# A steady block in a new order: the next block's early products in one group among the output products instead of two

## The chip, the cores and the metric

The kernel runs on one core of one Trainium2 chip. The metric is device time in microseconds of one execution on that core. Before the change three runs gave 2297.81, 2297.93 and 2298.03 us, so the median is 2297.93 us. One further execution was profiled; all durations below come from it.

## The reference

The input `x` is 8 sequences of 4096 tokens with 192 channels. First a causal convolution over 7 taps runs along each sequence, with one set of 7 softmax weights for each of 8 heads of 24 channels. Its result is 32768 tokens of 192 channels, which go through two matrix products with a SiLU between them. All of it is float32.

```python
w = np.exp(w); w = w / (np.sum(w, axis=-1, keepdims=True) + 1e-09)
x_unf = x_pad[:, idx, :].reshape(B, S, K, H, group)
out = np.einsum('hk,bskhg->bshg', w, x_unf)
...
h = x @ w_in                        # 192 -> 2048
g = h * (1.0 / (1.0 + np.exp(-h)))
return (g @ w_out)                  # 2048 -> 192
```

## The kernel before

**Blocks.** The 32768 tokens are cut into 32 blocks of 1024, and each block into two halves of 512. Channels lie on partitions. The convolution of a block is done by ScalarE, which scales shifted copies of the input (`v` steps, lines 542 and 545), and by accumulating DMAs that GpSimd issues (line 546). DMAs issued by SyncE (`sp` steps, line 572) spread its result over both halves of the 128 partitions as the tile `dup`, and VectorE forms sums of it (`w` steps, `win`, lines 589 and 592).

**Input products.** The product with `w_in` has 192 = 3 x 64 rows to sum over, so each TensorE product uses a 64-row half of the array, 64\*128. The kernel does not multiply plainly: in 5 groups of three 128-column chunks, 15 products per group (`P0` to `P14`, line 684) on sums of inputs and of weights take the place of 18. The one chunk left over is done plainly (`L`, line 701). `P8.2` is product 8 of group 2. The upper and lower 64 rows, called A and B here, work at the same time; the order of products goes in pairs, one of A and one of B. In float32 each product is two passes, so a trace shows two matmul records for each.

**Chains.** The products of a group accumulate into three chains, each in a PSUM bank of its own (`CHAINS`, `CHAIN_BANKS`). In the middle of a chain its value is read out. A `u` step (ScalarE copy, line 733) takes chain 0; an `X`, `a` or `b` step (VectorE add or subtract, line 727) takes chain 1 or 2. The next product of that chain may start only when the read is done. For instance chain 0 is products 5, 2, 6, 1, 0, 14, and `u4` copies it after product 2, so product 6 waits for `u4`. Chain 1 is products 3, 9, 7, 4, 8, and `a1` reads it after product 4, so product 8 waits for `a1`. `S` steps apply SiLU (ScalarE, line 745).

**Output products.** The product with `w_out` has 20 products `Q0` to `Q19`, each for 4 slices of its sum (line 820), on sums of `g` that VectorE and GpSimd form (`t` steps, line 809). They use column halves of the array, 128\*64, again two at a time. Copies and sums combine them (`O`, `C`, `d` on ScalarE, lines 855 and 857; `m` on VectorE, line 868), VectorE turns the result (`o`, line 876), SyncE stores it (`st`, line 884).

**The order.** The string `PLAN` lists the steps of one steady block, and the loop at line 1096 goes through it once for each block `b`. A sign ahead of a step moves it to another block: `-` is block b-1, `=` b-2, `~` b-3, `+` b+1, `*` b+2, none is b itself. Every instruction is pinned, so each engine runs its own steps in the order of this string, and waits on semaphores hold back the one at its head. `START` and `FINISH` list the steps of the first and last blocks. Most of block b-1's input products stand in the first half of the string, its output products in the second half. Ten of block b's products come early: `P5.4 P5.0 L.00 P2.4 P2.0 P3.4 P6.4 L.01 L.02 P6.0`. In the steady order of before, TensorE's own steps are: 76 input products (73 steps, since three `L.1x` steps make two each; the last three are P5.4, P5.0 and `-P8.2`, with P5.4 two steps ahead of P5.0), 8 output products, 4 input products (L.00, P2.4, P2.0, P3.4), 16 output products, 4 input products (P6.4, L.01, L.02, P6.0), 56 output products. Each place where input and output products meet is called a switch here; there are six in a block.

Of the kernel before, what the change touches and what calls it, by code (L numbers as in the profile page):

```python
# [17 lines left out]
def kernel(  # L18
# [59 lines left out]


    PLAN = (  # L80
# [24 lines left out]
    )  # L105
    START = (
# [20 lines left out]
    )  # L127
    QUEUE = (0, 4, 1, 2, 3)
    CHAIN_BANKS = (
        (5, 4, 2, 3, 3),  # L130
        (7, 5, 0, 1, 6),
        (0, 6, 4, 7, 2),
    )
    XBANKS = {
        2: (1, 1, 4, 7, 0),
        4: (1, 0, 6, 6, 0),
    }
    PLAIN_BANKS = (0, 0, 2)
    OUT_BANKS = {"DX": 7, "DY": 2, "D2": 1, "D3": 4, "DC": 2}

    def pin(ins):
        return tc.keep_in_program_order(ins)
# [211 lines left out]
    def combine(g, e):  # L354
# [47 lines left out]
        (("x", 3), ("o", 0), "-", ("x", 1)),  # L402
        (("o", 10), ("o", 9), "-", ("o", 10)),
        (("o", 9), ("o", 9), "-", ("x", 3)),
        (("o", 11), ("o", 11), "+", ("o", 9)),
        (("x", 4), ("o", 8), "-", ("o", 11)),
        (("o", 3), ("o", 0), "+", ("o", 3)),
        (("o", 0), ("o", 0), "+", ("o", 7)),
        (("x", 5), ("o", 6), "+", ("x", 4)),
        (("o", 6), ("o", 6), "-", ("o", 0)),  # L410
        (("o", 5), ("o", 5), "+", ("o", 8)),
        (("x", 7), ("o", 2), "+", ("x", 1)),
        (("o", 8), ("o", 1), "-", ("o", 8)),
        (("o", 2), ("o", 2), "+", ("o", 8)),
        (("o", 7), ("o", 7), "n", ("o", 7)),
        (("o", 10), ("o", 11), "-", ("o", 10)),
        (("x", 6), ("o", 3), "-", ("x", 4)),
        (("x", 0), ("x", 0), "n", ("x", 0)),
    )
    OUT_FORMS = {  # L420
# [187 lines left out]
    def rows(t, e):  # L608
        return t[R * e : R * e + R]
# [54 lines left out]
    def plain_bank(b, i):  # L664
        return banks[PLAIN_BANKS[i]]

# [144 lines left out]
    def out_bank(node):  # L811
        name, e = OUT_HOME[node]
        return rows(banks[OUT_BANKS[name]], e)

# [15 lines left out]
    def mid(i):  # L830
        if not mids:
            cmb = xpool.tile([P, 4, TB], F32, tag="cmb", name="cmb")
            mids.extend(cmb[:, c, :] for c in range(4))
            mids.extend(xpool.tile([P, TB], F32, tag="yx", name="yx", bufs=2) for _ in range(2))
            mids.append(xpool.tile([P, TB], F32, tag="m4", name="m4"))
        return mids[i]
# [22 lines left out]
    def out_sum(b, i):  # L859
# [4 lines left out]
            lambda: (out_bank("Y"), rows(mid(2), 1)),  # L864
            lambda: (banks[OUT_BANKS["D3"]], mid(1)),
            lambda: (banks[OUT_BANKS["D2"]], mid(0)),
        )[i]()
# [264 lines left out]
```

## Time and profile before

| What | Before |
|---|---|
| Median of 3 runs | 2297.93 us |
| The profiled execution's own time | 2298.43 us |
| Span of its instructions on the core | 2296.4 us |
| Mean granted TensorE clock | 0.999 |
| DMA engines, mean rate over the span | 106 GB/s |

The span runs from the first to the last instruction, and the rest of the execution's time lies around it. In the timeline each row has the start, the length (from the first start to the last end where several instructions are merged), the engine, the source line, the operation and what it writes and reads. Matmul records are 0.59 us long but start 0.43 us after one another on a half of the array, as they are pipelined. So starts are to be compared, not ends. PEld is the loading of weights for a matmul.

### The profile page before, as it was taken

How to read it: one execution, taken by the hardware profiler on the slowest of the kernel's cores; microseconds unless marked ns; L12 is line 12 of the kernel's file. 1: busy time of each engine (PE TensorE's matmuls, PEld its weight loads, DVE VectorE, ACT ScalarE, POOL GpSimd, SP SyncE). 2: the span in 40 equal slices, each digit the busy share in tenths (PEclk: the TensorE clock that was granted, in tenths of full speed). 3: DMA queues.
4: the chain of work that ended last, by engine and by line, in shares of the span. 5: the costliest groups of instructions: out<-in, count | busy, mean ns of one | idle time of the engine just before them, and what ended most of it. 6: DMA issues, size and time to landing. Idle time of an engine off the chain costs nothing.

```text
span 2296.4 us, 31730 instructions
## 1 busy us (share of the span) xinstructions
PE 2288.8 (100%) x10622; PEld 930.8 (41%) x10622; DVE 2004.8 (87%) x2265; ACT 1554.2 (68%) x2842; POOL 656.2 (29%) x734
## 2 busy tenths in 40 slices
PE   9999999999999999999999999999999999999998
PEld 4344433344433444333444334443345443344433
DVE  8888889888888988889888889888898888898887
ACT  6377766677666776667776667766677766677543
POOL 5762222322223322223222232222232222322200
PEclk9999999999999999999999999999999999999999
DMA  7665566755567665667655676656676557765411
GB/s 166 106 108 101 98 104 118 131 105 104 95 117 128 117 106 96 108 118 128 106 101 95 121 129 111 105 98 110 120 126 105 96 99 124 129 108 94 75 30 19
DMA packets 527139, 244.22 MB, mean 106 GB/s; under 512 B 431936, under 2 KB 437056, under 8 KB 526976
## 3 DMA queue, kind: packets, MB, share of 16 engines
q0 software_dynamic: 76480, 140.02, 35.9%
q1 hardware_dynamic: 446272, 101.65, 24.9%
q8 instruction: 84, 1.38, 0.2%
q10 hardware_dynamic: 4224, 0.52, 0.2%
q14 instruction: 79, 0.65, 0.1%
HBM read 31.46 MB, written 25.17 MB: 25 GB/s over the span
## 4 chain that ended last, share of the span: by engine, by line
PE 100%; DVE 0%; issue 0%; ACT 0%; ACTq 0%
PE ps L820 47%; PE ps L684 45%; PE ps L701 3%; PE ps L901 2%; PE ps L625 2%; PE ps L1010 1%; PE ps L463 0%; DVE yx L876 0%; DVE cmb L868 0%; ACT u L733 0%; PE ps L489 0%; DVE zeros L149 0%; DVE warm L149 0%; ACTq L733 0%; ACT g L750 0%
## 5 line engine op out<-in xcount | busy, mean ns | idle before, releaser
L546 POOL DMA_DIRECT2D nat<-u x528 | 453.0, 930 | 1238.6 <-ACT u L545 798.8
L820 PE MATMUL ps<-g,wall 128*64 128x512 f32 x1984 | 743.8, 596 | 0.0
L684 PE MATMUL ps<-win,wr 64*128 64x512 f32 x1550 | 684.7, 598 | 0.0
L684 PE MATMUL ps<-win,ws 64*128 64x512 f32 x1550 | 644.1, 592 | 0.3 <-ACT u L733 0.3
L733 ACT COPY u<-ps 128x512 f32<-128x512 f32 x775 | 439.5, 590 | 114.7 <-issue 58.9
L820 PE MATMUL ps<-g,wx 128*64 128x512 f32 x1240 | 415.2, 593 | 0.0
L684 PE MATMUL ps<-dup,wr 64*128 64x512 f32 x868 | 401.4, 590 | 0.0
L820 PE MATMUL ps<-t,wall 128*64 128x512 f32 x992 | 369.2, 594 | 0.0
L545 ACT ACTIVATE u<-xt,taps 128x512 f32<-128x512 f32 x528 | 357.7, 716 | 0.7
L684 PEld LDWEIGHTS ps<-win,wr 64*128 64x128 f32 x1550 | 256.8, 186 | 215.3 <-issue 129.1
L727 DVE TENSOR_TENSOR g<-u,ps 128x512 f32<-128x512 f32 x465 | 309.5, 682 | 32.1 <-PE ps L684 29.9
L820 PEld LDWEIGHTS ps<-g,wall 128*64 128x64 f32 x1984 | 216.0, 137 | 222.3 <-issue 213.0
L684 PEld LDWEIGHTS ps<-win,ws 64*128 64x128 f32 x1550 | 257.3, 187 | 119.4 <-issue 92.2
L745 ACT ACTIVATE g<-g 128x512 f32<-128x512 f32 x465 | 280.9, 631 | 34.4 <-DVE g L727 34.4
L745 ACT ACTIVATE g<-ps 128x512 f32<-128x512 f32 x465 | 279.9, 602 | 29.2 <-PE ps L684 28.5
L727 DVE TENSOR_TENSOR ps<-u,ps 128x512 f32<-128x512 f32 x310 | 214.9, 693 | 92.7 <-ACT u L733 33.7
L684 PE MATMUL ps<-dup,ws 64*128 64x512 f32 x682 | 270.1, 590 | 0.0
L820 PE MATMUL ps<-t,wx 128*64 128x512 f32 x744 | 267.3, 595 | 0.0
L809 DVE TENSOR_TENSOR t<-g 128x512 f32<-128x512 f32 (+1 forms) x186 | 240.9, 1309 | 4.3
L855 ACT COPY cmb<-ps 64x512 f32<-64x512 f32 x124 | 72.1, 581 | 236.4 <-PE ps L820 210.0
L809 DVE TENSOR_TENSOR t<-g,t 128x2048 f32<-128x2048 f32 x93 | 212.9, 2289 | 8.0 <-PE ps L820 6.8
L820 PEld LDWEIGHTS ps<-g,wx 128*64 128x64 f32 x1240 | 129.6, 137 | 211.0 <-issue 210.1
(103 smaller groups left out, 2477.0 us busy)
## 6 DMA issues: line engine op xcount, KB each, us to landing
nat<-u POOLq DMA_DIRECT2D x528, 256.0 KB, 4.2
dup<-nat SPq DMA_DIRECT2D x345, 128.0 KB, 2.5
nat<-in_x_dram SPq DMA_DIRECT2D x382, 64.0 KB, 3.9
out_dram<-yx SPq DMA_DIRECT2D x244, 64.0 KB, 2.2
out_dram<-cmb SPq DMA_DIRECT2D x122, 64.0 KB, 4.5
raw<-in_moe_w_out_dram SPq DMA_DIRECT2D x8, 384.0 KB, 4.4
g<-in_moe_w_in_dram SPq DMA_DIRECT2D x8, 192.0 KB, 5.5
ws<-wr POOLq DMA_DIRECT2D x8, 192.0 KB, 5.2
```

The lines of the kernel that those rows point to most:

```text
L545: pin(nc.scalar.activation(z, src, AF.Copy, scale=tap))
L546: pin(nc.gpsimd.dma_start(out=dst, in_=z, accum_op=ALU.add))
L625: nc.tensor.matmul(hs[a, n, e], rows(wr[j], e)[:, a, k, :], rows(d, e)[:, n, k, :], start=k == 0, stop=k == NK - 1,)
L684: nc.tensor.matmul(to[:, cols], raw(g, *LEFT[e][r], e), rhs[:, cols], start=first, stop=True, skip_group_check=True,)
L701: nc.tensor.matmul(plain_bank(b, n and 1 + e)[:, cols], rows(wr[j] if own == e else ws[j], e)[:, a, k, :], rows(dups[b], e)[:, SLOT[e][2 * ...
L727: pin(nc.vector.tensor_tensor(out_, u, v, op=op))
L733: pin(nc.scalar.copy(us[b, g, o][:, cols], t1[:, cols]))
L745: pin(nc.scalar.activation(h, src, AF.Silu))
L809: pin(engine.tensor_tensor(g_part(to, js), g_part(u, js), g_part(v, js), op=op))
L820: nc.tensor.matmul(out_bank(node), out_form(OUT_FORMS[r])[:, j, :], g_part(OPERAND[r], j), start=first, stop=True, skip_group_check=True,)
L855: pin(nc.scalar.copy(to(), out_bank(node)))
L901: nc.tensor.matmul(banks[DOWN_BANKS[k]][R * n : R * n + R, :], wo[j][:, a, e, R * k : R * k + R], g_tile(b, j, a)[:, n, e, :], start=j == ...
```

## The change

`PLAN` is a new order of the same 331 steps. In TensorE's order, the input products of a block now stand as 76 and 8: L.00 moves into the long section, `-P8.2` out of it into the short one, and the 4 + 4 early products of before become one group of 8 with it. The output products stand as 8 and 72 instead of 8, 16 and 56. The signs of many steps change with it, because the point of the string at which a block begins lies elsewhere. The `t`, `v`, `S`, `d`, `m`, `o` and `sp` steps are in new places too. Some chains, `X` sums, the plain chunk and two output sums get other PSUM banks. Three sums of output weights, formed once per run, are in a new order. `START`, `FINISH` and the functions are as they were. The diff, cut to the places where input and output products meet in the order, and the banks:

```diff
     PLAN = (
...
-        "-P11.2 -P10.3 -S1.1 -b1.2 -S3.3 -P4.2 -P8.3 -S1.3 -S0.1 -b5.3 -P10.2 P5.4 sp.0 -S1.0 "
-        "-S3.2 sp.2 -a1.2 P5.0 -a0.3 -S5.3 -b5.2 -P8.2 -Q4.3 -S1.2 +v.04 -Q17.1 -Q17.3 -Q4.2 "
-        "-a0.2 +v.15 -S5.2 -S4.2 -Q4.1 u5.0 -Q17.2 -tC4 w.0 u5.4 -Q4.0 -Q17.0 -O.0 L.00 w.1 "
-        "-C.0 P2.4 -tC3 -tD2 P2.0 P3.4 +v.23 +v.02 u4.0 u4.4 -S0.2 -Q5.1 -Q16.3 -Q3.2 -Q16.0 "
...
-        "+v.05 -Q6.2 +v.13 -t6 -Q16.2 -t5 -d.H -Q3.3 -Q12.0 *ld.0 -t7 +v.06 -t8 P6.4 L.01 -O.1 "
-        "-t9 L.02 P6.0 -Q6.1 -Q18.2 -Q15.2 -Q18.3 -Q15.1 -Q18.0 -Q11.3 -Q15.0 -t10 -Q13.1 "
...
+        "-u0.2 -P0.3 -tB1 -P9.2 -a1.1 -S2.3 -a5.3 -S5.1 -P0.2 -P11.3 -tC2 -P8.1 -u1.3 -S2.2 "
+        "-P12.3 -S1.0 -a0.1 -u1.2 -P14.3 -X4.2 -b1.3 -P14.2 -S0.0 -S1.1 -P12.2 -S4.3 sp.1 "
+        "-P4.3 -P7.2 -P11.2 -S3.2 -S3.3 +v.20 -b1.2 -P10.3 P5.4 -a1.3 -S4.2 -a5.2 -P10.2 -b5.3 "
+        "=st.2 -P8.3 -b5.2 -S5.3 sp.0 u5.4 -P4.2 sp.2 L.00 -a1.2 -a0.3 -S5.2 -S1.3 P5.0 u5.0 "
+        "+v.23 -Q4.1 -Q17.0 -Q4.3 -tC3 w.0 +v.14 -S0.1 -Q17.2 -Q17.3 -Q4.2 +v.01 -S1.2 w.1 "
+        "-Q17.1 -tD2 -Q4.0 -C.0 -P8.2 P2.4 -tC4 u4.4 L.01 P2.0 u4.0 P6.4 L.02 P6.0 P3.4 -O.0 "
+        "-Q3.3 -Q12.0 -Q5.0 -tD4 u2.0 -Q12.1 -tD3 +v.16 -Q12.2 +v.26 -S0.3 -a0.2 *ld.1 -Q5.1 "
...
     CHAIN_BANKS = (
-        (5, 4, 2, 3, 3),
-        (7, 5, 0, 1, 6),
-        (0, 6, 4, 7, 2),
+        (3, 4, 5, 2, 5),
+        (7, 3, 4, 1, 6),
+        (0, 6, 7, 0, 0),
     )
     XBANKS = {
-        2: (1, 1, 4, 7, 0),
-        4: (1, 0, 6, 6, 0),
+        2: (1, 1, 0, 7, 0),
+        4: (1, 0, 3, 6, 2),
     }
-    PLAIN_BANKS = (0, 0, 2)
-    OUT_BANKS = {"DX": 7, "DY": 2, "D2": 1, "D3": 4, "DC": 2}
+    PLAIN_BANKS = (0, 0, 5)
+    OUT_BANKS = {"DX": 7, "DY": 2, "D2": 4, "D3": 1, "DC": 2}
```

More of the change, by code (lines that the diff above doesn't have):

```diff
@@ L404 @@
         (("o", 9), ("o", 9), "-", ("x", 3)),
+        (("o", 5), ("o", 5), "+", ("o", 8)),
         (("o", 11), ("o", 11), "+", ("o", 9)),
@@ L410 @@
         (("o", 6), ("o", 6), "-", ("o", 0)),
-        (("o", 5), ("o", 5), "+", ("o", 8)),
         (("x", 7), ("o", 2), "+", ("x", 1)),
@@ L414 @@
         (("o", 2), ("o", 2), "+", ("o", 8)),
+        (("x", 6), ("o", 3), "-", ("x", 4)),
         (("o", 7), ("o", 7), "n", ("o", 7)),
         (("o", 10), ("o", 11), "-", ("o", 10)),
-        (("x", 6), ("o", 3), "-", ("x", 4)),
         (("x", 0), ("x", 0), "n", ("x", 0)),
```

35 rows, old and new, of the table PLAN are left out of this document.

## The prediction

> **What bounds the kernel now.** I read the page's busy shares first, then its chain of waits.
>
> ```profile
> span 2296.4 us, 31730 instructions
> PE 2288.8 (100%) x10622; PEld 930.8 (41%) x10622; DVE 2004.8 (87%) x2265; ACT 1554.2 (68%) x2842; POOL 656.2 (29%) x734
> PE 100%; DVE 0%; issue 0%; ACT 0%; ACTq 0%
> L505 DVE STREAM_TRANSPOSE xt<-nat 128x512 f32<-128x512 f32 x96 | 63.0, 682 | 0.6 <-DMA nat<-in_x_dram 0.6
> ```
>
> TensorE is busy all through, and the chain that ended last lies on it alone. The transposes count the blocks: 96, three each, so 32. No matmul is added or taken away by the change. So only time in which TensorE runs below its pace can be won, and I looked for it in the timeline of TensorE alone, at the places where input products (L684, L701) and output products (L820) meet. A half of the array starts a pass every 0.43 us there (1057.16 to 1059.73 are six steps, 0.428 each), whatever the kind of product. The columns are start and length in us, engine, line, operation. The first stretch holds the end of the long input section with P8.2, and the second the group L.00, P2.4, P2.0, P3.4.
>
> ```profile
> 1054.68 0.59 PE L684 MATMUL ps<-dup,ws 64*128 64x512 f32 x1
> 1055.11 0.59 PE L684 MATMUL ps<-dup,ws 64*128 64x512 f32 x1
> 1055.12 1.02 PE L684 MATMUL ps<-dup,wr 64*128 64x512 f32 x2
> 1055.63 0.69 PE L684 MATMUL ps<-win,wr 64*128 64x512 f32 x1
> ...
> 1056.68 0.64 PE L820 MATMUL ps<-t,wall 128*64 128x512 f32 x1
> 1057.16 0.59 PE L820 MATMUL ps<-t,wall 128*64 128x512 f32 x1
> ...
> 1059.73 0.59 PE L820 MATMUL ps<-t,wall 128*64 128x512 f32 x1
> 1060.26 0.69 PE L701 MATMUL ps<-dup,ws 64*128 64x512 f32 x1
> 1060.80 0.59 PE L701 MATMUL ps<-dup,ws 64*128 64x512 f32 x1
> 1061.23 0.59 PE L684 MATMUL ps<-win,ws 64*128 64x512 f32 x1
> 1061.66 0.59 PE L684 MATMUL ps<-win,ws 64*128 64x512 f32 x1
> 1062.18 0.64 PE L820 MATMUL ps<-t,wx 128*64 128x512 f32 x1
> 1062.66 0.59 PE L820 MATMUL ps<-t,wx 128*64 128x512 f32 x1
> ```
>
> The starts tell two losses. Around a group of input products, from 1059.73 to 1062.66, are six steps of one half: 2.93 us, where six times 0.43 are 2.57. **A switch there and back costs 0.36 us**: 0.10 and 0.10 on the way to input products (0.53, 0.54 in place of 0.43), 0.09 and 0.05 on the way back (0.52, 0.48).
>
> At P8.2, from 1055.11 to 1057.16, are four steps that should take 0.43 + 0.43 + 0.52 + 0.48 = 1.86 us; they take 2.05. **P8.2 loses 0.19 us**: its first pass starts at 1055.63 in place of 1055.55, 0.08 late, and is itself 0.69 in place of 0.59 long, 0.10 more. What it waits for is on VectorE and in the weight loads:
>
> ```profile
> 1054.26 0.59 PE L684 MATMUL ps<-win,ws 64*128 64x512 f32 x1
> 1054.89 1.29 DVE L727 TENSOR_TENSOR g<-u,ps 128x512 f32<-128x512 f32 x2
> 1055.63 0.29 PEld L684 LDWEIGHTS ps<-win,wr 64*128 64x128 f32 x2
> 1053.39 0.59 PE L684 MATMUL ps<-dup,ws 64*128 64x512 f32 x1
> 1053.69 0.32 PEld L684 LDWEIGHTS ps<-win,wr 64*128 64x128 f32 x2
> 1053.82 0.59 PE L684 MATMUL ps<-win,wr 64*128 64x512 f32 x1
> L727 DVE TENSOR_TENSOR g<-u,ps 128x512 f32<-128x512 f32 x465 | 309.5, 682 | 32.1 <-PE ps L684 29.9
> L684 PEld LDWEIGHTS ps<-win,wr 64*128 64x128 f32 x1550 | 256.8, 186 | 215.3 <-issue 129.1 <-ACT u L733 43.8 <-ACT g L750 13.3
> ```
>
> P4.2's last pass starts at 1054.26 and ends at 1054.85; the first of the two sums, `a1.2`, starts at 1054.89, and is done 0.68 later (the mean in its group's row is 682 ns) at 1055.57; the weights are loaded from 1055.63. Only one pair of products lies between, and the handoff takes 0.59 + 0.04 + 0.68 + 0.06 = 1.37 us from pass to pass, where the slot comes after three steps, 1.29. The load at 1053.69 is out of step too, yet 0.13 us ahead of its matmul at 1053.82; that one starts in step (0.43 after 1053.39) and nothing is lost. So a late handoff costs its lateness, and up to 0.10 more when the load has no lead; with a lead of 0.13 it costs nothing.
>
> **The change part by part.**
>
> *One group in place of two.* By the order of TensorE's instructions, a steady block now has input sections of 76 and 8 products, output sections of 8 and 72: four switches in place of six. Over the program 188 such changes become 128, so 30 returns are saved: 30 x 0.36 = 10.8 us, all of it on TensorE's own path.
>
> *P8.2 goes to the early group.* Now P5.0, eight output products and a switch lie between `-a1.2` and `-P8.2`: the handoff of 1.37 us has some 4 us. It is no longer late, in 30 blocks: 30 x 0.19 = 5.7 us. Sixteen blocks later the same rows stand in the timeline:
>
> ```profile
> 2180.98 0.59 PE L684 MATMUL ps<-dup,ws 64*128 64x512 f32 x1
> 2182.55 0.64 PE L820 MATMUL ps<-t,wall 128*64 128x512 f32 x1
> 2183.03 0.59 PE L820 MATMUL ps<-t,wall 128*64 128x512 f32 x1
> ```
>
> It is 2.05 us from 2180.98 to 2183.03 again, and the block's period is (2182.55 - 1056.68) / 16 = 70.37 us.
>
> *A new short handoff.* In one group, P2.4, `u4.4`, P6.4 stand with one pair (L.01, P2.0) between, and P2.0, `u4.0`, P6.0 likewise with (P6.4, L.02); before, 16 output products lay between. The reader is ScalarE's copy, not VectorE's sum:
>
> ```profile
> 1036.23 0.59 PE L684 MATMUL ps<-win,ws 64*128 64x512 f32 x1
> 1036.86 0.58 ACT L733 COPY u<-ps 128x512 f32<-128x512 f32 x1 [0.48 <-PE ps L684]
> L733 ACT COPY u<-ps 128x512 f32<-128x512 f32 x775 | 439.5, 590 | 114.7 <-issue 58.9 <-PE ps L684 53.3
> ```
>
> A pass from 1036.23 ends at 1036.82, the copy starts 0.04 later and takes 0.585. With 0.06 to the load (P8.2's row) that is 0.59 + 0.04 + 0.58 + 0.06 = 1.27 us, and the slot is at 1.29. So the load comes with a lead of some 0.02. No row has this lead: with none the pass grew by 0.10, with 0.13 by nothing. So the price is 0 to 0.10 a block, nearer to the row without lead: I take 0.10 - 0.02 = 0.08. The second handoff comes after the same delay on its own half, so it has a lead of 0.02 + 0.08 and is free. 30 x 0.08 = 2.4 us (0 to 3).
>
> The Trainium skill bears on this term (TensorE: Matmul & The Clock Gate, LDWEIGHTS): a load takes its columns divided by 1.2 in ns, an estimate of 107 ns for 128 columns, while the mean load record in the group's row is 186 ns long. The pass that grew by 0.10 agrees with the page, not with the record's length; by the record, 0.19 - 0.02 a block, the term would be 5 us and the sum 2288.
>
> *A second one.* -P7.2 now comes three pairs after P8.1 with two VectorE sums between that stand in each other's way (`-a0.1`, then `-X4.2`, which writes the bank that `-a0.1` reads): 0.59 + 0.05 + 0.68 + 0.68 + 0.06 = 2.06 us against five steps, 2.14. A lead of 0.08 lies between the two rows: 0 to 0.02 a block; I take 0.01, 0.3 us.
>
> *The other steps.* By the order, no other reader of a chain has fewer products to cover it than the shortest of before that shows no loss. A step's place in the string matters on its own engine's queue alone. On SyncE's, the loads of ld.1 and the stores of st.3 no longer stand ahead of sp.0 and sp.2, but those of st.2 do; VectorE turns their data in the string's first fifth. The last spread waits for -P10.2, and from that to P2.4 are 13 products, 12 before. On GpSimd's, tA1 has 26 products, 11 us, until -Q4.1 reads its sum. The `t`, `v`, `d`, `m` and `o` steps lie beside 72 output products; VectorE and ScalarE have slack over the span (87% and 68%). The three output-weight sums are once per run on GpSimd, busy 29%, beside the first input products. I take nothing for these; if that cover is gone it is the third rival.
>
> *The last block.* It has no next block, so P5.4, L.00 and P5.0 drop out and -P8.2 follows -P4.2 directly. The 1.37 us handoff then meets the very next slot at 0.43: 0.94 late and 0.10 more, against 0.19 there now. +0.9 us (0 to 1.5), once.
>
> **The sum**, against the profiled execution's own time of 2298.43 us: 2298.43 - 10.8 - 5.7 + 2.4 + 0.3 + 0.9 = 2285.5. The median of the runs is 0.5 lower than that execution, so I say **2285.2 us** for the runs. With the bounds of the unknown terms, 2298.4 - 16.5 - 0.5 + (0 to 5.1) is 2281.4 to 2286.5. Rows are read to 0.01 us, and 0.02 a block is 0.6 us, so its own range is 2281 to 2287.
>
> **The rivals.**
>
> *ScalarE comes late to the copy u4.4 (slower).* The copies of the four early chains now fall in one short stretch, behind the steps u5.0, three `v`, two `S` and C.0. Busy times in the eight output products of before (length, then PE, PEld, DVE, ACT), and rows of ScalarE in it:
>
> ```profile
> 1056.68:1060.26 3.58, 3.58 (x17) 1.06 (x16) 3.52 (x6) 3.36 (x7) 1.72 (x2) 1.00 0.73 136
> 1056.77 1.32 ACT L545 ACTIVATE u<-xt,taps 128x512 f32<-128x512 f32 x2
> 1058.99 1.06 ACT L733 COPY u<-ps 128x512 f32<-128x512 f32 x2
> ```
>
> For it: ScalarE is busy 3.36 of 3.58 us there. Against: two scalings take 1.32, two copies 1.06, so in a row a scaling adds about 0.6 us, a copy 0.5, a SiLU by estimate the same. The seven steps add 0.5 + 3 x 0.6 + 2 x 0.5 + 0.5 = 3.8 us (C.0 taken as a copy), and from P5.0's end to P2.4's end are 8 + 2 passes and two switches, 4.6. So ScalarE has 0.8 us to spare, or 0.6 after C.0, which must wait for -Q4.0. It decides from a lateness of 0.6 us; above that P6.4 is late by the rest, plus 0.10. The change is lost when this eats (10.8 + 5.7 - 0.9) / 30 = 0.52 a block, so from 1.0 us. Two scalings, 1.2 us, slipping in ahead of the copy would make 0.6 + 0.1 = 0.7 a block: 2298.4 + 21 - 15.6 - 0.5, a time of **2303**. The Trainium skill's PSUM Bottleneck (TensorEngine Tiling (Array Packing), Performance Considerations) speaks for it: tiling speeds TensorE but not the reading of PSUM. The trace agrees so far as ScalarE's 3.36 of 3.58 goes, not on the chain of waits.
>
> *The late handoff moves.* P8.2's loss of 0.19 goes, but another reader (VectorE has 13% to spare, and sums of two groups are nearer to each other) is as late each block. Then only the switches are won: 2298.4 - 10.8 + 2.4 + 0.9 - 0.5 = 2290.4. For it: the distances of one pair. Against: the two that I found have leads.
>
> *The time saved is waited out elsewhere*, in the 72 output products, where VectorE's `t` sums feed the next product: TensorE then stands 0.5 us a block there, and the time stays at 2294 to 2300. Against, the view of who waited for whom (us in total, times, longest):
>
> ```profile
> PEld ps L820 <- DVE t L809: 0.9, 1, 0.9
> ```
>
> TensorE waited for a `t` sum once.
>
> **How the numbers follow.** The forecast has 0.60, the moved handoff 0.16, the even time 0.08, ScalarE late 0.10; 0.06 is left for a gain above the forecast's (no exposed load, more slack: 2281 and less). A change under 0.2%, 4.6 us, can't be told from none. Faster: 0.60 + 0.16 + 0.06 and 0.02 of the even case, 0.84. Same: 0.06. Slower: 0.10. The range 2279.5 to 2294 holds the forecast, the moved handoff and part of the even case; the late ScalarE stays out.
>
> **What would show it.** TensorE's timeline of a steady block: two groups of input products, the short one with eight; each there and back still 0.36; P8.2's first pass in step after the switch; P6.4's first pass 0.59 to 0.69 long with a load that waited for ACT u L733; 70.37 - 0.36 - 0.19 + 0.09 = 69.9 us from block to block. I am wrong if matmuls of L684 or L820 start out of step at other places, if the load of P6.4 comes more than 0.1 us behind its slot, or if the waits name `t` or `win` ahead of TensorE.

## The result, and the profile after

The changed kernel takes 2294.24 us, the median of 20 runs (2291.62 to 2295.58). The kernel before, run on the same chips, takes 2298.10 us (2297.69 to 2299.68, 20 runs). The ratio is 0.9982, with a 95% interval of 0.9975 to 0.9989. So the change gains 3.9 us; the forecast was a gain of 12.9, to 2285.2 us.

The page of the changed kernel, its span, its busy shares and the shares of its chain of waits:

```profile
span 2292.1 us, 31941 instructions
PE 2281.2 (100%) x10622; PEld 922.3 (40%) x10622; DVE 1998.9 (87%) x2265; ACT 1560.2 (68%) x2842; POOL 655.6 (29%) x734
PE 99%; DVE 1%; issue 0%; ACT 0%; DVEq 0%
```

TensorE is still the whole chain but for 1%, which is now VectorE's; it was 0% before. The shares of the other engines say nothing about where 9 us stayed away. The block's period does. From the trace of each kernel I take the start of the same product in successive blocks: the median of 28 differences is 70.344 us before and **70.150 us** after. That is 0.194 a block less, where 0.46 was forecast (0.36 + 0.19 - 0.09).

TensorE's timeline of one steady block of the changed kernel, with ScalarE's copies and the weight loads, in the places where the prediction looked before (start and length in us, engine, line, operation, what it writes and reads, how many merged, and in brackets the idle time before it and who ended it):

```profile
1054.38 0.59 PE L701 MATMUL ps<-dup,ws 64*128 64x512 f32 x1
1054.90 0.64 PE L820 MATMUL ps<-t,wall 128*64 128x512 f32 x1
1055.38 0.59 PE L820 MATMUL ps<-t,wall 128*64 128x512 f32 x1
...
1057.96 0.59 PE L820 MATMUL ps<-t,wall 128*64 128x512 f32 x1
1058.49 1.13 PE L684 MATMUL ps<-win,wr 64*128 64x512 f32 x4
1059.69 0.58 ACT L733 COPY u<-ps 128x512 f32<-128x512 f32 x1 [0.19 <-PE ps L684]
1059.88 1.14 PE L684 MATMUL ps<-win,wr 64*128 64x512 f32 x2
1060.32 0.18 PEld L684 LDWEIGHTS ps<-win,wr 64*128 64x128 f32 x1 [0.68 <-ACT u L733]
1060.33 0.69 PE L701 MATMUL ps<-dup,ws 64*128 64x512 f32 x1
1060.86 0.59 PE L684 MATMUL ps<-win,wr 64*128 64x512 f32 x1
```

The switches cost what they did: 0.53 from 1057.96 to 1058.49 into the group, 0.52 and 0.48 out of the long section (1054.38, 1054.90, 1055.38), where 0.43 is the pace. P8.2, now the first of the group, is in step. P6.4 is not. Its copy starts at 1059.69 and lasts 0.58, so the weights are loaded at 1060.32. The slot was 1059.88 + 0.43 = 1060.31, so the load has no lead. P6.4's first pass is merged into the row of 1059.88, its second starts at 1060.86; the row of 1060.33 is L.02, its partner on the other half, whose load comes behind P6.4's and which is held with it. The passes at 1060.33 and 1060.86 are 0.02 late and 0.53 apart in place of 0.43. P6.4 costs 0.12 a block.

The other losses stand in the long section, where the prediction had put next to nothing. First P7.2, in the same view:

```profile
1048.27 0.59 PE L684 MATMUL ps<-win,wr 64*128 64x512 f32 x1
1048.94 0.69 DVE L727 TENSOR_TENSOR g<-u,ps 128x512 f32<-128x512 f32 x1 [0.19 <-PE ps L684]
1049.67 0.69 DVE L727 TENSOR_TENSOR ps<-u,ps 128x512 f32<-128x512 f32 x1
1050.41 0.18 PEld L684 LDWEIGHTS ps<-win,wr 64*128 64x128 f32 x1 [0.24 <-DVE ps L727]
1050.42 0.69 PE L684 MATMUL ps<-win,wr 64*128 64x512 f32 x1
1050.42 1.02 PE L684 MATMUL ps<-win,ws 64*128 64x512 f32 x2
...
1054.28 0.59 PE L684 MATMUL ps<-dup,wr 64*128 64x512 f32 x1
1054.38 0.59 PE L701 MATMUL ps<-dup,ws 64*128 64x512 f32 x1
```

P8.1's pass is at 1048.27, `a0.1` follows at 1048.94 and `X4.2` at 1049.67. P7.2's weights are loaded at 1050.41, its slot is 1050.42. With no lead its first pass is 0.69 long, and half A runs 0.10 behind half B from there (1054.38 beside 1054.28) until the switch, which waits for both halves: 0.10 a block.

Then a stretch earlier in the long section, with VectorE's rows:

```profile
1030.17 0.69 DVE L727 TENSOR_TENSOR g<-u,ps 128x512 f32<-128x512 f32 x1
1030.78 1.30 DVE L876 STREAM_TRANSPOSE yx<-cmb 128x512 f32<-128x512 f32 x2
1030.92 0.30 PEld L684 LDWEIGHTS ps<-win,wr 64*128 64x128 f32 x4 [0.58 <-DVE g L727]
1031.00 1.05 PE L684 MATMUL ps<-win,wr 64*128 64x512 f32 x4
1032.00 0.65 DVE L727 TENSOR_TENSOR g<-g,ps 128x512 f32<-128x512 f32 x1
1032.31 0.59 PE L684 MATMUL ps<-win,ws 64*128 64x512 f32 x1
1032.70 0.18 PEld L701 LDWEIGHTS ps<-dup,ws 64*128 64x128 f32 x1 [0.63 <-DVE g L727]
1032.75 0.66 PE L701 MATMUL ps<-dup,ws 64*128 64x256 f32 x2
```

`a5.4`, the two transposes `o.3` and `o.2`, and `b5.4` stand back to back on VectorE. By the chains it is P4.4 that waits for `a5.4`; P7.0, its partner on the other half, is held with it, and one of the recorded expectations below names this place by P7.0. The load comes 0.08 ahead of its slot (1030.92, 1031.00), and 0.02 is lost. L.11 writes the bank that `b5.4` reads: its load comes 0.04 ahead (1032.70; the slot is 1032.31 + 0.43), and 0.07 is lost. P11.4, which adds to the bank that `X4.4` writes, loses 0.02 in the same way, and P12.4 beside it.

So a block pays 0.123 + 0.10 + 0.070 + 0.024 + 0.023 = 0.34 us for five handoffs that were free before or did not exist, against 0.355 saved on the switches and 0.187 on P8.2: net 0.20, and 0.194 was measured.

The rest comes once per run. I cut the trace into TensorE's input and output sections and subtract the number of steps times 0.429 us from each section's length. What is left is its loss:

| Loss over TensorE's pace, us | Before | After |
|---|---|---|
| 29 long input sections | 12.27 | 13.03 |
| early groups (60; 30) | 13.02 | 9.83 |
| of these, the first of block 1 alone | 1.07 | 0.33 |
| output sections among them (90; 60) | 13.93 | 9.45 |
| first long section of the steady order (block 1) | 2.14 | 4.61 |
| the run's first input section | 3.23 | 2.51 |
| the last long section | 1.26 | 2.36 |
| the last output section | 2.41 | 2.19 |

The rows of the long input sections, the early groups and the output sections among them fall by 6.9 us; the last four rise by 2.6. The difference, 4.3, is that of the spans. Not all of the 6.9 is steady: the first early group of the kernel before lost 1.07 us, a later one 0.20, so 0.9 of it comes once. Block 1's long section loses 2.5 more, and the last block, without a next one, 1.1 (forecast 0.9). The 0.7 of the first input section lies in the start ahead of it, and is not the change's: `START` is the same, and this row is between 2.3 and 3.3 us in the traces of all the kernels of this document, without order.

### The profile page after: what moved, and what is told of

Its sections match the earlier page's. It is cut to its first block, busy times and chain, and to the rows that moved or that the text cites. A ratio compares the mean times of both kernels' runs of the same rounds, so it can differ in the third digit from the quotient of the medians.

```text
span 2292.1 us, 31941 instructions
## 1 busy us (share of the span) xinstructions
PE 2281.2 (100%) x10622; PEld 922.3 (40%) x10622; DVE 1998.9 (87%) x2265; ACT 1560.2 (68%) x2842; POOL 655.6 (29%) x734
## 4 chain that ended last, share of the span: by engine, by line
PE 99%; DVE 1%; issue 0%; ACT 0%; DVEq 0%
PE ps L820 47%; PE ps L684 45%; PE ps L701 3%; PE ps L901 2%; PE ps L625 2%; PE ps L1010 1%; PE ps L463 0%; DVE g L727 0%; DVE ps L727 0%; DVE g L809 0%; DVE t L809 0%; DVE xt L505 0%; DVE yx L876 0%; DVE cmb L868 0%; DVE u L727 0%
## 5 line engine op out<-in xcount | busy, mean ns | idle before, releaser
L820 PE MATMUL ps<-g,wall 128*64 128x512 f32 x1984 | 757.9, 594 | 0.0
L684 PE MATMUL ps<-win,wr 64*128 64x512 f32 x1550 | 656.0, 600 | 2.0 <-DVE ps L727 1.2
L820 PE MATMUL ps<-g,wx 128*64 128x512 f32 x1240 | 389.6, 592 | 0.0
L727 DVE TENSOR_TENSOR g<-u,ps 128x512 f32<-128x512 f32 x465 | 307.8, 683 | 48.7 <-PE ps L684 46.6
L684 PEld LDWEIGHTS ps<-win,wr 64*128 64x128 f32 x1550 | 243.1, 186 | 246.7 <-issue 120.6
L820 PEld LDWEIGHTS ps<-g,wall 128*64 128x64 f32 x1984 | 226.1, 137 | 223.6 <-issue 199.9
L855 ACT COPY cmb<-ps 64x512 f32<-64x512 f32 x124 | 72.0, 581 | 334.2 <-PE ps L820 276.2
L684 PE MATMUL ps<-dup,ws 64*128 64x512 f32 x682 | 296.1, 589 | 0.0
L684 PEld LDWEIGHTS ps<-win,ws 64*128 64x128 f32 x1550 | 246.1, 186 | 123.1 <-issue 60.3
L745 ACT ACTIVATE g<-ps 128x512 f32<-128x512 f32 x465 | 263.1, 608 | 2.9 <-PE ps L684 2.9
L820 PE MATMUL ps<-t,wx 128*64 128x512 f32 x744 | 252.0, 594 | 0.0
L727 DVE TENSOR_TENSOR ps<-u,ps 128x512 f32<-128x512 f32 x310 | 210.8, 689 | 44.8 <-ACT u L733 16.8
L809 DVE TENSOR_TENSOR t<-g 128x512 f32<-128x512 f32 (+1 forms) x186 | 240.1, 1318 | 3.3
L809 DVE TENSOR_TENSOR t<-g,t 128x2048 f32<-128x2048 f32 x93 | 210.2, 2287 | 1.2
L820 PEld LDWEIGHTS ps<-g,wx 128*64 128x64 f32 x1240 | 121.5, 137 | 211.4 <-issue 194.2
```

Source lines behind the costliest of these rows:

```text
L684: nc.tensor.matmul(to[:, cols], raw(g, *LEFT[e][r], e), rhs[:, cols], start=first, stop=True, skip_group_check=True,)
L727: pin(nc.vector.tensor_tensor(out_, u, v, op=op))
L745: pin(nc.scalar.activation(h, src, AF.Silu))
L809: pin(engine.tensor_tensor(g_part(to, js), g_part(u, js), g_part(v, js), op=op))
L820: nc.tensor.matmul(out_bank(node), out_form(OUT_FORMS[r])[:, j, :], g_part(OPERAND[r], j), start=first, stop=True, skip_group_check=True,)
L855: pin(nc.scalar.copy(to(), out_bank(node)))
```

## The experiments

The theory after this reading: the switches and P8.2 gave what was forecast, and five short handoffs took 0.34 us a block back. The rival that matters most: VectorE (87% busy) or ScalarE is short of time as such, the five places are only where it shows, and a loss that is cured turns up at the next reader. All periods below are medians over the steady blocks of a run's trace, read as above.

**One reader made shorter, then all of them.** A sum or copy over 384 columns is done earlier (0.48 in place of 0.58 for the copy, 0.56 in place of 0.69 for the sum); a quarter of its columns is left out.

```diff
-            cols = columns(half)
+            cols = slice(0, 384) if b > 2 and (name, g) in (('u4', 4), ('u4', 0)) else columns(half)
```

> The changed kernel, but from block 3 on the copies u4.4 and u4.0 take 384 of their 512 columns, so P6.4's and P6.0's weights can be loaded some 0.15 us earlier (a quarter of these two copies is left out). Theory (five handoffs with too little lead eat the gain; P6.4's is 0.123 us a block): the block's period falls from 70.15 to 70.03 us, P6.4 starts in step, and the time is 2294.2 - 30 x 0.123 = 2290.5 us. Rival (the engines that read PSUM are short of time as a whole, and a loss that is cured turns up at the next reader): the period stays at 70.15, the time at 2294.

```diff
-            pin(nc.vector.tensor_tensor(out_, u, v, op=op))
+            k = slice(0, 384) if b > 2 and (name, g) in (('X4', 2),) else slice(0, TB); pin(nc.vector.tensor_tensor(out_[:, k], u[:, k], v[:, k], op=op))
```

> The changed kernel, but from block 3 on the sum X4.2, for which P7.2 waits, takes 384 of its 512 columns (a quarter of it is left out). Theory: P7.2's half no longer lags by 0.10 us, the period falls from 70.15 to 70.05 us and the time to 2294.2 - 30 x 0.10 = 2291.2 us. Rival (the loss turns up at the next reader): 70.15 and 2294.

The fourth has both edits, with the list `u4.4, u4.0, X4.2, X4.4, X4.0, a5.4, b5.4`:

> The changed kernel, but from block 3 on all the reads that the five handoffs wait for (u4.4, u4.0, X4.2, X4.4, X4.0, a5.4, b5.4) take 384 of their 512 columns; a quarter of these seven steps is left out. Theory: all five losses go, 0.123 + 0.10 + 0.07 + 0.024 + 0.023 = 0.34 us a block; period 69.81 us, time 2294.2 - 10.2 = 2284.0 us, which is about what was predicted for the change. Rival (loss turns up elsewhere): the fall is much smaller than the sum of the three single ones. Rival (a switch is worth less than 0.36 us): the period falls by less though all places are in step, and the four switches take over 0.71 us a block.

**One reader moved in its queue**, nothing shortened:

```diff
-... -w.4 -a5.4 =o.3 =o.2 -b5.4 -P4.4 ...
+... -w.4 -a5.4 =o.3 -b5.4 =o.2 -P4.4 ...
```

> The changed kernel, but VectorE does b5.4 ahead of the second of the two transposes o.3 and o.2 in place of behind both; nothing is left out. b5.4 is done 0.6 us earlier, and L.11, which shares its bank, no longer waits. Theory: the 0.07 us at L.11 goes, period 70.08 us, time 2294.2 - 2.1 = 2292.1 us. Rival (the loss turns up at the next reader of VectorE, for instance P8.4 behind a1.4): 70.15 and 2294. If the bank that L.11 shares with b5.4 were not the cause, L.11 stays 0.07 out of step.

| Run | Period, us | Time, us | Ratio to before (95%) |
|---|---|---|---|
| the changed kernel | 70.150 | 2294.24 | 0.9982 (0.9975 to 0.9989) |
| e1_copies_short | 70.042 | 2291.07 | 0.9967 (0.9955 to 0.998) |
| e2_x42_short | 70.048 | 2291.01 | 0.9968 (0.9956 to 0.998) |
| e3_b54_first | 70.067 | 2291.37 | 0.9969 (0.9958 to 0.9981) |
| e4_all_short | 69.826 | 2284.95 | 0.994 (0.9928 to 0.9953) |

Each cure took off what that place had cost: 0.108, 0.102 and 0.083 a block (0.123, 0.10 and 0.07 expected), and all together 0.324. The loss did not move on. In e4_all_short the losses left in a steady block are the four switches, 0.20 + 0.15 twice, and 0.02 at P6.4 and L.02: with the handoffs gone, the two gains are all there. That its 2284.95 us is so near the forecast of 2285.2 is luck: the period falls by 0.518 in place of 0.46, because the forecast still paid 0.09 for P6.4 and P7.2, and block 1 takes more back than the forecast knew of (its long section loses 4.30 us against 2.14 before, its first early group 0.33 against 1.07).

The timeline of e1_copies_short at the place of P6.4 shows why 0.02 stays (the rows of L701 are again L.02, beside P6.4):

```profile
1059.35 0.48 ACT L733 COPY u<-ps 128x384 f32<-128x384 f32 x1 [0.19 <-PE ps L684]
1059.88 0.18 PEld L684 LDWEIGHTS ps<-win,wr 64*128 64x128 f32 x1 [0.57 <-ACT u L733]
1059.97 0.61 PE L701 MATMUL ps<-dup,ws 64*128 64x512 f32 x1
1060.42 0.59 PE L701 MATMUL ps<-dup,ws 64*128 64x512 f32 x1
```

The load has a lead of 0.09 now, the pass is in step at 1059.97, and the next comes after 0.45 in place of 0.43.

**The gains by themselves, from the kernel before.** First P8.2's reader alone: the edit of e2 on the kernel before, with `('a1', 2)` in the list, so that a quarter of that sum is left out.

> The kernel before, but from block 3 on the sum a1.2, for which P8.2 waits, takes 384 of its 512 columns (a quarter of it is left out). It is done some 0.17 us earlier. Theory: of P8.2's 0.19 us a block 0.17 to 0.19 go, period 70.344 - 0.18 = 70.16 us, time 2298.2 - 30 x 0.18 = 2292.8 us. Rival (the late handoff moves to the next reader): period 70.34, time 2298.

Measured: 70.212 us, 2294.82 us, ratio 0.9985 (0.9977 to 0.9994). The period falls by 0.132, less than the 0.17 to 0.19 expected; the missing 0.05 is still at P8.2, as the timeline of this kernel shows:

```profile
1053.80 0.18 PEld L684 LDWEIGHTS ps<-win,wr 64*128 64x128 f32 x1 [0.19 <-DVE g L727]
1053.85 0.65 PE L684 MATMUL ps<-win,wr 64*128 64x512 f32 x1
```

I had taken the shorter sum to be done 0.17 earlier; it is 0.13. The lead is 0.05, the pass grows to 0.65, and 0.05 is paid. Nothing else moved out of step, so the loss does not move to another reader.

Then the merge alone, with the banks and the long section of before:

```diff
-... P2.4 -tC3 -tD2 P2.0 P3.4 +v.23 +v.02 u4.0 u4.4 -S0.2 -Q5.1 -Q16.3 -Q3.2 -Q16.0 ...
+... P2.4 u4.4 -tC3 -tD2 P2.0 P3.4 u4.0 P6.4 L.01 L.02 P6.0 +v.23 +v.02 -S0.2 -Q5.1 -Q12.1 -Q3.2 -Q12.0 ...
```

> The kernel before with one thing changed: P6.4, L.01, L.02, P6.0 follow P3.4 at once, so six switches a block become four; u4.4 and u4.0 go up with them, and in the output section the Q12 products go ahead of the Q16 products, with O.1 behind them, so that no t sum comes late. Banks, the long section and P8.2 stay. Nothing is left out. Theory: a switch there and back is worth 0.355 us, and the new short handoff at P6.4 takes 0.12 of it back: period 70.344 - 0.355 + 0.12 = 70.11 us, time 2298.2 - 30 x 0.235 = 2291.2 us; P8.2 still loses 0.19. Rival (a return is worth much less than 0.36, and the change's gain is P8.2's alone): period 70.34 or more, time 2298 or more. Rival (ScalarE or VectorE gets short of time when the group is merged): output products out of step, period above 70.3.

Measured: 70.231 us, 2293.81 us, ratio 0.9982 (0.9973 to 0.9991). The fall is 0.113, half of what was expected. ScalarE's and TensorE's rows of f2_merged:

```profile
1059.02 0.56 ACT L855 COPY ps<-ps 64x512 f32<-64x512 f32 x1 [0.36 <-PE ps L820]
1059.60 0.57 ACT L857 ACTIVATE ps<-ps 64x512 f32<-64x512 f32 x1
1060.19 1.29 ACT L733 COPY u<-ps 128x512 f32<-128x512 f32 x2
1060.83 0.18 PEld L684 LDWEIGHTS ps<-win,wr 64*128 64x128 f32 x1 [0.80 <-ACT u L733]
1060.84 0.69 PE L701 MATMUL ps<-dup,ws 64*128 64x512 f32 x1
```

O.0 (L855) waits for its output product and ends at 1059.58, C.0 (L857) at 1060.17, and only then comes `u4.4`, at 1060.19. P2.4's second pass had started at 1059.42 and ended at 1060.01, so the copy starts 0.18 after its end, where 0.08 was usual, and P6.4 loses 0.241 in place of 0.12. Without that, the section losses of this run add up to a saving of 0.354 on the switches: 0.113 + 0.241. ScalarE as a whole has slack; a single step in front of the copy is what costs. The next run moves that step:

```diff
-... -Q4.0 -Q17.0 -O.0 L.00 w.1 -C.0 P2.4 u4.4 -tC3 -tD2 P2.0 P3.4 u4.0 P6.4 ...
+... -Q4.0 -Q17.0 L.00 w.1 -C.0 P2.4 u4.4 -tC3 -tD2 P2.0 P3.4 u4.0 -O.0 P6.4 ...
```

> As f2_merged (the kernel before with P6.4, L.01, L.02, P6.0 moved up into the other group), and O.0 moves behind u4.0. In f2_merged ScalarE did O.0 and C.0 just ahead of u4.4, the copy began 0.15 us after it could have, and P6.4 lost 0.241 us a block. Nothing is left out. Theory (the price of a handoff is its lateness plus 0.105): u4.4 begins at once, P6.4 loses 0.12, period 70.231 - 0.118 = 70.11 us, time 2293.8 - 3.5 = 2290.3 us. Rival (ScalarE is short of time around the group): O.0 now delays u4.4's followers or the Q16 products, and the period stays at 70.2.

And P8.2's reader shortened on top of it:

> As f3_merged_o0, and from block 3 on a1.2 takes 384 of its 512 columns (a quarter of it is left out), as in f1_a12_short. This has the prediction's two gains and P6.4's handoff, and none of the other new places of the changed kernel. Theory (what was missing to the forecast were the handoffs that the rest of the new order made): period 70.11 - 0.133 = 69.98 us, time 2290.3 - 4.0 = 2286.3 us, 8 us below the changed kernel. Rival (VectorE or ScalarE is the bound as soon as TensorE gains): period above 70.05.

| Run | Period, us | Time, us | Ratio to before (95%) |
|---|---|---|---|
| f3_merged_o0 | 70.116 | 2290.49 | 0.9966 (0.9953 to 0.9978) |
| f4_merged_a12 | 69.983 | 2286.78 | 0.995 (0.9937 to 0.9962) |

Both are as expected (70.11 and 2290.3; 69.98 and 2286.3). The copy and the load in the timeline of f3_merged_o0:

```profile
1058.13 0.58 ACT L733 COPY u<-ps 128x512 f32<-128x512 f32 x1 [0.47 <-PE ps L684]
1058.77 0.18 PEld L684 LDWEIGHTS ps<-win,wr 64*128 64x128 f32 x1 [0.68 <-ACT u L733]
```

The copy now waits for TensorE (0.47), not for its own queue, and the load is as late as in the changed kernel (the section losses give 0.12). f3_merged_o0 leaves nothing out, keeps P8.2's loss of 0.19, and is still 3.8 us faster than the changed kernel, which does not have that loss. Of this, 30 x 0.034 = 1.0 us is in the steady blocks, so there the rest of the new order took more than P8.2's cure brought; by the section losses, block 1's long section (2.40 here) gives 2.2 and the last one (1.27) 1.1, and the first early group (1.25 here) takes 0.9 back.

**A version that keeps the change and moves three VectorE steps:**

```diff
-... =m.1 =m.5 +i.0 ... =m.3 -X4.4 -X4.0 ... -P10.4 -w.4 -a5.4 =o.3 =o.2 -b5.4 ... *i.2 w.3 -Q8.1 u2.4 -m.4
+... =m.5 +i.0 ... =m.3 -X4.4 =m.1 -X4.0 ... -P10.4 -a5.4 =o.3 -b5.4 =o.2 ... *i.2 w.3 w.4 -Q8.1 u2.4 -m.4
```

> The changed kernel with three moves in VectorE's order and nothing left out: b5.4 stands between o.3 and o.2; w.4 stands at the end of the block before, behind w.3, so that a5.4 starts earlier; m.1 stands behind X4.4, so that X4.4 starts earlier. Theory: the losses at L.11 (0.07), at P7.0 (0.023) and at P12.4 (0.024) go, those at P7.2 and P6.4 stay: period 70.15 - 0.117 = 70.03 us, time 2294.2 - 3.5 = 2290.7 us. Rival (VectorE is the bound of this stretch, a reader that is served earlier makes another one late): period 70.07 or above.

Measured: 70.024 us, **2288.11 us**, ratio 0.9958 (0.9946 to 0.9971). The period is as expected. VectorE's timeline in that stretch:

```profile
1026.88 0.70 DVE L876 STREAM_TRANSPOSE yx<-cmb 128x512 f32<-128x512 f32 x1
1028.03 0.69 DVE L727 TENSOR_TENSOR g<-g,ps 128x512 f32<-128x512 f32 x1 [0.44 <-PE ps L684]
1028.63 0.70 DVE L876 STREAM_TRANSPOSE yx<-cmb 128x512 f32<-128x512 f32 x1
```

`b5.4` (1028.03) now waits for TensorE, with 0.44 to spare, where it had stood behind both transposes. P12.4, P7.0 and L.11 are in step; P7.2 and P6.4 pay as before. This is the fastest version of all that leave nothing out: 9.7 us below the kernel before, 6.1 below the changed one. Of the 6.1, the steady blocks give 30 x 0.126 = 3.8; most of the rest is block 1, whose long section loses 2.16 us in the profiled run in place of 4.61. The five runs spread from 2287.20 to 2290.36 us, so the 2.3 beyond the steady blocks is less sure than the 3.8.

**Block 1.** The timelines of VectorE and GpSimd in block 1. L809 are `g` sums, on GpSimd `tA1` over 1536 columns, on VectorE first `tB1` over 512 and then `tC2` over 1024; L149 are the sums of output weights, on GpSimd. The kernel before:

```profile
133.68 1.25 DVE L809 TENSOR_TENSOR g<-g,t 128x1024 f32<-128x1024 f32 x1
133.80 1.71 POOL L149 TENSOR_TENSOR wall<-zeros,wall 128x256 f32<-128x256 f32 x1
```

The changed kernel:

```profile
128.28 3.54 POOL L809 TENSOR_TENSOR t<-g 128x1536 f32<-128x1536 f32 x1
131.17 2.57 DVE L809 TENSOR_TENSOR t<-g 128x512 f32<-128x512 f32 x1
132.48 0.71 POOL L149 TENSOR_TENSOR wx<-wall,wx 128x256 f32<-128x256 f32 x1
133.67 1.27 DVE L727 TENSOR_TENSOR g<-u,ps 128x512 f32<-128x512 f32 x2
134.86 2.23 DVE L809 TENSOR_TENSOR g<-g,t 128x1024 f32<-128x1024 f32 x1
135.13 0.87 POOL L149 TENSOR_TENSOR wx<-zeros,wx 128x256 f32<-128x256 f32 x1
```

And e5_reordered:

```profile
131.82 1.14 DVE L809 TENSOR_TENSOR t<-g 128x512 f32<-128x512 f32 x1
132.34 1.21 POOL L149 TENSOR_TENSOR wall<-wall 128x256 f32<-128x256 f32 x1
134.07 1.24 DVE L809 TENSOR_TENSOR g<-g,t 128x1024 f32<-128x1024 f32 x1
```

In a steady block `tB1` takes 0.69 and `tC2` 1.22. In block 1 of the changed kernel they take 2.57 and 2.23, and each ends about its own length after a run of GpSimd's sums has ended (133.74 after 133.19, where the run began with `tA1`; 137.09 after 136.00); the sums that read PSUM (L727, two in 1.27) are not slower. In the other two kernels it is mostly GpSimd whose sum is long (1.71, 1.21); in e5_reordered `tB1` takes 1.14. P7.2, behind `tC2`, `a0.1` and `X4.2`, stood 1.40 us in the changed kernel's block 1. Two runs tried to avoid the meeting by moving `tB1` in block 1 alone:

```diff
-        for t in plan:
-            step(b, t)
+        for t in first if b == 2 else plan: step(b, t)
```

where `first` is the plan with `-tB1` ahead of `-tA1` (h1), or ahead of `-a1.2` (h2, and e6 on top of e5_reordered).

> The changed kernel, but in block 1 alone VectorE's sum tB1 stands ahead of GpSimd's tA1, as in the kernel before; all other blocks are as in the changed kernel. In block 1 tB1 took 2.57 us and tC2 2.23 us beside GpSimd's sums, where a steady block has 0.69 and 1.22, and P7.2 then stood 1.40 us. Theory (this collision makes the head's first section lose 2.5 us more than before): tB1 takes 0.7 to 0.8 us, P7.2's wait in block 1 falls below 0.4 us, the time falls by about 1 us, to 2293.2. Rival (the wait in block 1 comes from the order of the products alone): P7.2 waits 1.4 us as it did, and the time stays.

> The changed kernel, but in block 1 alone VectorE does tB1 after b5.2, when GpSimd's sums of the output weights are done. In the changed kernel and in e3_b54_first tB1 began while GpSimd's tA1 still ran and took 2.57 us; in e5_reordered it took 1.14 us and the first section lost 2.5 us less. Theory (that meeting of VectorE and GpSimd is the head's extra loss): tB1 takes about 0.7 us, P7.2 in block 1 no longer stands for 1.4 us, the head's section of 80 products loses 2.2 to 3.2 us in place of 4.6, time 2294.2 - 1.4 to 2.4 = 2291.8 to 2292.8 us. Rival (tC2, the next sum over two operands in SBUF, meets GpSimd in its place): P7.2 still waits over 1 us, time 2294.

> e5_reordered (three moves in VectorE's order, nothing left out) and, in block 1 alone, tB1 after b5.2. Theory: the steady period stays at 70.025 us and the head does not get worse whichever way the meeting of VectorE and GpSimd falls: 2287 to 2288.5 us, faster than both kernels. Rival (e5_reordered's good head was the lucky side of that meeting and moving tB1 spoils it): 2289 to 2291.

| Run | Loss of block 1's long section, us | Period, us | Time, us | Ratio to before (95%) |
|---|---|---|---|---|
| the changed kernel | 4.61 | 70.150 | 2294.24 | 0.9982 (0.9975 to 0.9989) |
| h1_tb1_first | 4.86 | 70.150 | 2296.09 | 0.9993 (0.9984 to 1.0001) |
| h2_tb1_later | 4.95 | 70.142 | 2294.10 | 0.9979 (0.997 to 0.9987) |
| e5_reordered | 2.16 | 70.024 | 2288.11 | 0.9958 (0.9946 to 0.9971) |
| e6_best | 4.75 | 70.024 | 2289.90 | 0.9962 (0.9949 to 0.9976) |

Neither move helped. In h1_tb1_first `tB1` met GpSimd all the same and took 2.91 us, with P7.3 standing 2.4 us. (Its runs lie between 2294.5 and 2299.0 us and the profiled one at the lower end, so its median holds something that this trace does not show.) In h2_tb1_later `tC2` met GpSimd instead, as that rival said:

```profile
133.79 3.85 DVE L809 TENSOR_TENSOR g<-g,t 128x1024 f32<-128x1024 f32 x1
134.29 0.89 POOL L149 TENSOR_TENSOR wall<-zeros,wall 128x256 f32<-128x256 f32 x1
134.99 0.88 POOL L149 TENSOR_TENSOR wall<-wall 128x256 f32<-128x256 f32 x1
135.67 0.88 POOL L149 TENSOR_TENSOR wx<-zeros,wx 128x256 f32<-128x256 f32 x1
```

In e6_best it was `tC2` too, 3.79 us long. In the five traces of this table the section loses 4.6 us and more where VectorE's sum is the one that stands, and 2.2 where GpSimd's is. So I read e5_reordered's good block 1 as the favourable side of that meeting and no merit of its three moves; e6_best, with the same steady blocks, is 1.8 us slower (1.0 when each is taken against the kernel before as run beside it: e6_best is 8.7 us below, e5_reordered 9.7). An order in which GpSimd has finished the sums of the output weights by then wasn't tried, so that the meeting is the whole of the 2.5 us stays an inference from these traces.

## Why the prediction came out as it did

**Right: the switches.** Forecast 0.36 a return, measured 0.355 in the changed kernel and 0.354 in f2_merged, where the groups were merged and the long section and the banks stayed.

**Right: P8.2.** It is in step in its new place, and the 0.187 is gone.

**Right: the last block**, 0.9 forecast, 1.1 measured. 0.2 of the 1.1 are the other handoffs there: in e4_all_short, without them, that section loses 2.17 us in place of 2.36.

**Mis-sized: P6.4.** The mechanism is the one described, the lead was not. The copy starts 0.08 after the pass has ended in place of 0.04 (P2.4's second pass is in the merged row, 1058.49 + 0.53 + 0.59 = 1059.61; the copy starts at 1059.69), so the load is some 0.02 late, not 0.02 early: 0.123 a block in place of 0.08, 1.3 us more over the run.

**Mis-sized: P7.2**, forecast "A lead of 0.08 lies between the two rows: 0 to 0.02 a block; I take 0.01". From pass to load it is 1050.41 - 1048.27 = 2.14 us, not 2.06: 0.08 in place of 0.05 from the pass to `a0.1`, 0.04 between the two sums, which were added as if back to back, and 0.01 each on the sums. The lead is nil, the price 0.10: 2.7 us over the run. The bound of 0.02 was the real mistake. The rows said that a lead of 0.13 costs nothing and no lead 0.10, and nothing in between; a term with an uncertain 0.08 in it should have kept 0 to 0.10.

**The step that failed: the other steps.** "By the order, no other reader of a chain has fewer products to cover it than the shortest of before that shows no loss." That counts products on TensorE. It leaves out what stands ahead of the reader in its own queue. At the start of the block the new order puts `i.0` and `w.4` among the sums on VectorE, and two transposes in place of one ahead of b5.4, so that X4.4, a5.4 and b5.4 are done late for about as many products to cover them as before (7, 5 and 4; before 6, 5 and 5). L.11, P4.4 with P7.0, and P11.4 with P12.4 lost 0.070 + 0.023 + 0.024 a block, 3.5 us over the run. e5_reordered, which moves three of VectorE's steps and none of TensorE's, took just these 0.12 off again. The sentence on slack over the span (87%) was no cover either: right ahead of a5.4 and b5.4 VectorE was busy back to back while the mean was not.

**Missed: block 1**, 2.5 us more in its long section, against 0.9 less in its first early group, whose loss before was not followed up. The prediction put the sums of the output weights beside the first input products on an engine that is 29% busy; the traces say that it matters when VectorE's sums meet them. (In the diff two of these sums stand elsewhere, not three.)

Together: 1.3 + 2.7 + 3.5 in the steady blocks, 2.5 - 0.9 in block 1, 0.2 in the last block, less 0.2 at the end, is 9.1; missing were 9.0.

**The rivals.** "The late handoff moves" named the kind of loss, though no single handoff as late as P8.2 came; five small ones did. ScalarE being late at u4.4 was the right place, but in the changed kernel ScalarE was not late: its copy waited for TensorE (the row of 1059.69), and the load was 0.02 late by the handoff's own length. In f2_merged, with one step more in front, ScalarE's queue was late, and the load by 0.14. No output product lost anything in a steady block, so nothing was waited out there. The Trainium skill's load time, an estimate of 107 ns for 128 columns (TensorE: Matmul & The Clock Gate, LDWEIGHTS), is borne out: the pass behind a load with no lead grows by 0.10 at P7.2 and at P6.4, not by the 0.18 of the load's record.

## What to carry to other kernels

A reordering that saves on one engine must be read on all of them: for each handoff, follow the pass, the wait in the reader's own queue, the read and the load, and compare the result with the slot; the count of products between two steps is not enough. Where the sum comes within 0.1 us of the slot, take the price from both bounds. When a kernel runs on a fixed pace, a table of each section's loss over that pace finds losses of 0.02 us a block that no busy share shows.

## What the runs showed of the hardware

**The price of a short lead was linear here.** Lead of the weight load ahead of its slot, and what the handoff then costs, over eight places of these traces:

| Place | Lead, us | Cost, us |
|---|---|---|
| P6.4 in e1_copies_short | 0.09 | 0.017 |
| P4.4 with P7.0, after | 0.08 | 0.023 |
| P11.4 with P12.4, after | 0.08 | 0.024 |
| P8.2 in f1_a12_short | 0.05 | 0.054 |
| L.11, after | 0.04 | 0.070 |
| P7.2, after | 0.00 | 0.10 |
| P6.4, after | -0.02 | 0.123 |
| P6.4 in f2_merged | -0.14 | 0.241 |

Cost and lead add up to 0.10 to 0.11 in every row.

**A VectorE sum with both operands in SBUF can stand while GpSimd sums**, for several GpSimd instructions on end: 0.69 became 2.57 and 2.91, 1.22 became 2.23 and 3.85. Sums with an operand in PSUM kept their 0.68. The Trainium skill says that such a VectorE instruction contends with a GpSimd instruction that reads SBUF, and that issue order decides who blocks (SBUF — State Buffer, Who interferes with whom). The traces agree on the contention. On the order they do not settle it: in h2_tb1_later VectorE's row starts at 133.79, 0.50 ahead of GpSimd's at 134.29, and still it is VectorE's that is long. The 3.85 spans three of GpSimd's sums, so as far as these rows show, the one that waits was not let in between two that follow each other.
